# A planner that keeps GpSimd's time, and a multiply that moves to GpSimd, in a two-layer attention and MLP kernel

## The chip, the cores and the metric

The kernel runs on one core of one Trainium2 chip. A core has five engines that run side by side: TensorE (PE in the profile; its weight loads are PEld), VectorE (DVE), ScalarE (ACT), GpSimd (POOL) and SyncE (SP), which here only issues DMAs. Each engine takes its instructions in order. They share the on-chip memory SBUF; matmuls write to the banks of PSUM, which VectorE and ScalarE read. The metric is the device time of one execution in microseconds; the time given for a kernel is the median of several.

## The reference

Two layers, each with attention and an MLP with the same weights, on x of 2048 x 512. LN is a norm without scale or shift.

```python
for _ in range(2):
    qkv = LN(x) @ wqkv                       # 512 -> 3 x 32 heads x 16
    p = softmax(q @ k^T * 16 ** -0.5)        # per head, 2048 x 2048
    x = x + (p @ v, heads side by side) @ wo
    x = x + silu(LN(x) @ w1) @ w2            # 512 -> 1792 -> 512
```

There are 2 layers x 32 heads x 2048 x 2048 exponentials, and no mask.

## The kernel before

**Tiling.** Scores are made transposed: 128 keys (a key tile, 16 of them) by 512 queries (a chunk `qc`, 4 of them). A *step* is one key tile of one head group (`g`, `par`), which has four heads; their four score matmuls have a contraction of 16 and lie in four row strips of the array, so they run at once. A *run* is the steps of one head group over its key tiles: 16, or fewer where `RUNS` splits them (in the first chunk of layer 0 four runs of 4 steps, as keys become ready; steps 1 to 128). There are 1024 steps.

**Exponentials.** They are shared out. Of a step's four blocks, ScalarE takes three (one instruction for one block, one for two, L1140), in tiles `p_sb`. The fourth, the block `d`, goes another way and is scored four steps ahead (`D_LEAD`): VectorE turns the scores `d_ps` into 16-bit integers `d_y` (L1058) that, read as fp16, are a rough exponential, and GpSimd adds two constants to a pair of them (`d_z`, L1078, two instructions for two steps). The three terms are multiplied with weighted values (`VA`, and `VB`, which GpSimd makes in `scale_v`, L559) and their sum is a closer exponential. The first 12 steps differ: there four blocks go to ScalarE.

**PV.** Every second step, `emit_pv` (L933) multiplies the exponentials with the values into one PSUM bank `o_ps`, in which a run's sum is kept, with a row of ones for the softmax's denominator. It decides which of the waiting terms of `d` blocks it takes: term y from one step after it was issued, the z terms from three and four steps after, all that are left at a run's end or when buffers (five pairs) would run out.

**A run's end.** VectorE copies `o_ps` to `oT` (L1038). For 45 of the 64 head groups (`by_dma`) an SP transpose brings it to `ot`; then VectorE takes the reciprocal of the denominators (`rec`, L601) and multiplies (L603) into `attn`. For the other 19, TensorE transposes into PSUM (`att`) and the same two instructions read that. When a chunk's groups are done, `out_proj` issues four SP transposes out of `attn` and background work begins: output projection, norm, MLP, next layer's keys, values and queries.

**The planner.** All engines' instruction streams are written in one order by the Python code. Beside the fixed stream of steps stand generators of background work (`Background`: `queue`, `side`, `outs`, `urgent`). Each yields a `Part` with its cost on TensorE (`pe`) or VectorE (`dve`) and a label it needs. `Model` keeps a clock for TensorE (`pe`), ScalarE (`act`), VectorE (`dve`) and SP (`sp`), and after each step's exponentials the loop issues every part that `fits`: one whose work ends, by the model, before ScalarE would miss its next scores. `done[label]` is the modelled time at which a label is ready. GpSimd has no clock in it. Of the norms, `ln_stats` issues statistics on VectorE and two GpSimd instructions for `rstd` (L396, L397), and `ln_chunk` applies them on VectorE (`xn`, L402), in three buffers, and transposes them by SP.

**Zero multiplications.** In a step with no other TensorE work, `fill(FILL)` issues three groups of four matmuls of zeros into the open `o_ps`, if the model has room. It can't do this when the newest accumulation has not been started in all four column strips or is finished. `warm(n)` makes n matmuls into a bank of the background (`bank`, one bank after step 5).

**Tail.** After the last step come the last chunk's output projection, norm and MLP, by hand (`tail`).

Of the kernel before, what the change touches and what calls it, by code (L numbers as in the profile page):

```python
# [28 lines left out]
class Background:  # L29
# [44 lines left out]
    def advance(self, item):  # L74
        if self.model:
            self.model.charge(item[2])
        try:
# [4 lines left out]
            else:  # L82
                home = [q for q in (self.outs, self.side, self.queue) if item in q][0]
                home.remove(item)
                self.done[item[0]] = self.model.landed if self.model else 0.0

    def heads(self, now):
        return [
            self.outs[0] if self.outs else None,
            self.head(now),  # L90
            self.prime(self.side[0]) if self.side else None,
        ]
# [17 lines left out]
class Model:  # L110
# [12 lines left out]
    TRANSPOSED = 1.7  # L123
    DMA = 0.64

    def __init__(self, slack, margin):
        self.slack, self.margin = slack, margin
        self.pe = self.act = self.dve = self.ready = self.free = 0.0
        self.s1 = self.sd = self.copied = self.sp = self.landed = 0.0
        self.s2 = [0.0, 0.0]  # L130
        self.mode = None
        self.early = False
        self.evacuated = 0.0
# [37 lines left out]
    def pv(self, groups):  # L171
        self.pe = max(self.pe, self.copied)
        self.to("V")
        self.pe += self.GROUP * groups
        self.summed = self.pe + self.TO_DVE

    def transpose(self):
# [41 lines left out]
def kernel(  # L219
# [10 lines left out]
    nc = tc.nc  # L230
# [188 lines left out]
    def ln_pair(c, i):  # L419

        stats[c, i] = yield from ln_stats(c, (i, i + 1))

    def ln_transpose(i, xns, dst, copy=nc.vector.tensor_copy):
# [9 lines left out]
    def ln_chunk(c, dst):  # L433

        for i in (0, 2):
            mv, rstd = stats.pop((c, i))
            for u in range(2):
                yield part(0.45, need=("xn", xn_count[0] - XN_BUFS))
# [112 lines left out]
    def scale_v(L, c):  # L551

        n = len(d_blocks(c))
        VB[L, c] = vbpool.tile([P, n * 2 * VBW + 16], FP16, name="VB", tag="VB", bufs=7)
        nc.gpsimd.memset(VB[L, c][:, n * 2 * VBW :], 0.0)
# [17 lines left out]
    def group_out(L, qc, pi, g, par, oT):  # L573
# [10 lines left out]
        else:  # L584
# [16 lines left out]
        nc.vector.reciprocal(rec[:], att[:, :, :, 16:17])  # L601
        yield part(0.43, held=not by_dma(L, qc, pi, g, par))
        nc.vector.tensor_tensor(  # L603
            out=attn[L, qc][:, :, P * g : P * (g + 1)].rearrange(
# [29 lines left out]
    def out_proj(L, qc):  # L634
        if (L, qc) == (0, 0):
            load_wo()
        aT = wo[0][:, CT : 2 * CT, :].rearrange("p t (c q) -> p t c q", c=CT)
        for i in range(4):
            transpose(aT[:, i, :, :], attn[L, qc][:, i, :])
# [311 lines left out]
    def emit_pv(t, mms):  # L951
# [20 lines left out]
        for d in list(d_todo):  # L972
# [3 lines left out]
            must = ends or d["pair"] <= last  # L976
            while d["rhs"] and (must or d["rhs"][0][0] <= t):
                if must:
                    _, k, rhs = d["rhs"].pop(0)
                    lanes[j].append(pv_block(d["blk"], k, rhs))  # L980
                else:
                    more[j].append((d, d["rhs"].pop(0)))
# [67 lines left out]
    def emit_d(t, blk):  # L1050
# [14 lines left out]
        )  # L1065
        d = dict(blk=blk, pair=len(pairs), left=NT)
        d["rhs"] = [(t + 1, 0, pr["y"][:, len(pr["ds"]), :].bitcast(FP16))]
        pr["ds"].append(d)
# [4 lines left out]
    def other_terms(t, pr):  # L1073

        n = len(pr["ds"])
        for k, (off, _) in enumerate(TERMS):
# [7 lines left out]
                op1=ALU.mult,  # L1084
            )
            for i, d in enumerate(pr["ds"]):
                d["rhs"].append((t + 3 + k, k + 1, z[:, i, :].bitcast(FP16)))

    def end_group(L, qc, pi, g, par):
# [13 lines left out]
    with tc.manual_schedule(  # L1103
# [62 lines left out]
        for t in range(1, len(steps)):  # L1166
# [19 lines left out]
            for i in range(n1):  # L1186
                score(a_blks[i], s1[i])
            if n1 == 1:
                for blk in d_blks:
                    emit_d(t, blk)  # L1190
            m.scores(len(a_blks), len(d_blks))
            while after:
# [37 lines left out]
            if not busy and m.fill_fits(FILL):  # L1230
                n = fill(FILL)
                if n:
                    m.pv(n)
        t = len(steps) + 1
        emit_pv(t, pv_step(t))
# [37 lines left out]
```

## Time and profile before

| what | value |
|---|---|
| time, median of 4 executions | 1566.27 us (1563.36 to 1567.93) |
| the profiled execution's own time | 1563.36 us |
| its span, first to last instruction | 1561.6 us |
| ScalarE busy | 1513.9 us, 97% |
| TensorE busy (matmuls; zeros included) | 1458.2 us, 93% |
| GpSimd busy | 1113.8 us, 71% |
| VectorE busy | 1080.3 us, 69% |
| mean granted TensorE clock | 0.993 |
| first exponential of the stream; last step's first | 14.2 us; 1518.8 us |

The busy time of ScalarE counts overlapping instructions once. A row of the profile's groups gives line, engine, operation, output and inputs, shapes and count, then busy time and mean length of one, then the idle time of the engine just before them and what ended it. What ended a wait is inferred: it is the event that came last. In rows of stages the columns are the stretch, its length, each engine's busy time with the number of instructions, the granted clock, the DMA engines' share and GB/s.

### The profile page before, as it was taken

How to read it: one execution, taken by the hardware profiler on the slowest of the kernel's cores; microseconds unless marked ns; L12 is line 12 of the kernel's file. 1: busy time of each engine (PE TensorE's matmuls, PEld its weight loads, DVE VectorE, ACT ScalarE, POOL GpSimd, SP SyncE). 2: the span in 40 equal slices, each digit the busy share in tenths (PEclk: the TensorE clock that was granted, in tenths of full speed). 3: DMA queues.
4: the chain of work that ended last, by engine and by line, in shares of the span. 5: the costliest groups of instructions: out<-in, count | busy, mean ns of one | idle time of the engine just before them, and what ended most of it. 6: DMA issues, size and time to landing. Idle time of an engine off the chain costs nothing. (4 is left out here: it accounts for less than half of the span.)

```text
span 1561.6 us, 34164 instructions
## 1 busy us (share of the span) xinstructions
PE 1458.2 (93%) x13284; PEld 465.2 (30%) x13361; DVE 1080.3 (69%) x1733; ACT 1513.9 (97%) x2191; POOL 1113.8 (71%) x1172
## 2 busy tenths in 40 slices
PE   7999998899998999899998999988999899999998
PEld 3222332222322322222222323322332232222225
DVE  6877677667776777667776677676677666676645
ACT  6999999999999999999999999999999999999993
POOL 2888777677876778667876778776777677776760
PEclk9999999999999999999999999999999999999999
DMA  4110013101121112201021010121012101120110
GB/s 138 32 28 2 5 36 65 31 23 37 45 47 27 35 22 52 52 18 39 21 49 43 10 35 9 24 58 32 18 46 62 32 18 29 45 48 22 38 45 14
DMA packets 149442, 55.84 MB, mean 36 GB/s; under 512 B 127776, under 2 KB 148768, under 8 KB 149280
## 3 DMA queue, kind: packets, MB, share of 16 engines
q1 hardware_dynamic: 149280, 53.65, 14.1%
q8 instruction: 105, 1.72, 0.5%
q14 instruction: 57, 0.47, 0.1%
HBM read 28.57 MB, written 4.19 MB: 21 GB/s over the span
## 5 line engine op out<-in xcount | busy, mean ns | idle before, releaser
L1140 ACT ACTIVATE p_sb<-s_ps 128x512 bf16<-128x512 f32 x2026 | 1467.0, 1104 | 7.3 <-PE d_ps L909 6.2
L1078 POOL TENSOR_SCALAR d_z<-d_y 128x1024 uint16<-128x1024 uint16 x1012 | 1058.0, 1045 | 366.6 <-DVE d_y L1058 179.2
L1058 DVE TENSOR_SCALAR d_y<-d_ps 128x512 uint16<-128x512 f32 x1012 | 696.9, 689 | 404.0 <-PE d_ps L909 360.4
L909 PE MATMUL s_ps<-QT,KT 32*128 32x512 bf16 x3084 | 631.1, 382 | 61.4 <-ACT p_sb L1140 45.1
L909 PE MATMUL d_ps<-QT,KT 32*128 32x512 bf16 x1012 | 389.8, 385 | 8.4 <-DVE d_y L1058 5.2
L909 PEld LDWEIGHTS <-KT 32*128 32x128 bf16 x4096 | 187.4, 91 | 647.8 <-issue 595.2
L933 PE MATMUL o_ps<-p_sb,VA 128*32 128x512 bf16 x3039 | 311.9, 388 | 8.0 <-DVE oB L1038 1.1
L933 PE MATMUL o_ps<-d_z,VB 128*32 128x512 f16 x2024 | 249.4, 381 | 0.0
L933 PE MATMUL o_ps<-d_y,VA 128*32 128x512 f16 x1012 | 153.4, 380 | 0.0
L933 PEld LDWEIGHTS <-VA 128*32 128x32 bf16 x4096 | 86.6, 95 | 159.6 <-issue 121.9
L466 PE MATMUL h_ps<-fT,w 128*128 128x512 bf16 x392 | 102.6, 382 | 8.4 <-DVE hT L652 6.6
L711 PE MATMUL f_ps<-w_sb,hT 128*128 128x512 bf16 x350 | 97.0, 382 | 4.1 <-issue 3.3
L933 PEld LDWEIGHTS <-VB 128*32 128x32 f16 x2024 | 78.5, 98 | 55.4 <-issue 0.5
L933 PE MATMUL o_ps<-w_qkv,zero 128*32 128x512 bf16 x1344 | 93.1, 383 | 0.0
L649 ACT ACTIVATE t_sb<-h_ps 128x512 f32<-128x512 f32 x98 | 86.7, 884 | 0.0
L652 DVE SCALAR_TENSOR_TENSOR hT<-t_sb,h_ps 128x512 bf16<-128x512 f32 x98 | 67.2, 686 | 22.8 <-ACT t_sb L649 22.6
L603 DVE TENSOR_TENSOR attn<-ot,rec 128x256 bf16<-128x256 bf16 x45 | 49.5, 1099 | 1.5
L1038 DVE CAST oT<-o_ps 128x512 bf16<-128x512 f32 x64 | 43.5, 680 | 7.7 <-PE o_ps L933 7.7
L466 PEld LDWEIGHTS <-w 128*128 128x128 bf16 x392 | 30.0, 97 | 55.1 <-issue 30.3
L402 DVE TENSOR_SCALAR xn<-x,mv,rstd 128x512 bf16<-128x512 bf16 x64 | 42.5, 677 | 3.5 <-POOL rstd L397 1.9
L392 DVE BATCH_NORM_STATS2 st<-x 128x6 f32<-128x512 bf16 x64 | 43.5, 680 | 2.0 <-DMA x<-in_A_x_dram 2.0
L711 PEld LDWEIGHTS <-hT 128*128 128x128 bf16 x392 | 29.2, 97 | 46.4 <-issue 25.0
(77 smaller groups left out, 613.8 us busy)
## 6 DMA issues: line engine op xcount, KB each, us to landing
w<-in_B_w_dram SPq DMA_DIRECT2D x100, 128.0 KB, 2.4
wo<-in_A_wo_dram SPq DMA_DIRECT2D x8, 512.0 KB, 3.7
QT<-q SPq DMA_DIRECT2D x240, 16.0 KB, 1.8
x<-in_A_x_dram SPq DMA_DIRECT2D x7, 512.0 KB, 4.2
x<-x SPq DMA_DIRECT2D x16, 128.0 KB, 1.8
x<-x SPq DMA_DIRECT2D x4, 512.0 KB, 3.7
out_dram<-x SPq DMA_DIRECT2D x16, 128.0 KB, 1.7
w_sb<-in_B_w_dram SPq DMA_DIRECT2D x1, 1792.0 KB, 13.5
```

The costliest lines, as they stand in the source:

```text
L392: nc.vector.bn_stats(st[:], x_sb[c][:, i, :])
L466: nc.tensor.matmul(ps.rearrange("p (t q) -> p t q", q=P) if len(r.shape) == 3 else ps, lhsT=lhs(ct), rhs=r, start=(ct == 0), stop=(ct == C ...
L603: nc.vector.tensor_tensor(out=attn[L, qc][:, :, P * g : P * (g + 1)].rearrange("p t (j s) -> p t j s", s=32)[:, :, :, 16 * par : 16 * par ...
L649: nc.scalar.activation(t_sb, h_ps, ACT.Tanh, scale=0.5)
L652: nc.vector.scalar_tensor_tensor(out=hT[:, ft, :], in0=t_sb, scalar=1.0, in1=h_ps, op0=ALU.add, op1=ALU.mult)
L711: nc.tensor.matmul(y_ps, lhsT=hT[:, ft, tq * P : (tq + 1) * P], rhs=w2_sb[:, ft, :], start=(ft == 0), stop=(ft == FT - 1),)
L909: nc.tensor.matmul(out, lhsT=KT[L, kt // 4][r, g, (kt % 4) * P : (kt % 4 + 1) * P], rhs=QT[g][r, par, :], start=True, stop=True,)
L933: nc.tensor.matmul(o_tiles[key][32 * j : 32 * j + 32, :], lhsT=lhsT, rhs=rhs, start=(o_count[key][j] == 0), stop=stop,)
L1038: nc.vector.tensor_copy(out=o, in_=o_tiles[key][:])
L1058: nc.vector.tensor_scalar(out=pr["y"][:, len(pr["ds"]), :], in0=s_ps[:], scalar1=float(1024 * SCALE * math.log2(math.e)), scalar2=float(10 ...
L1078: nc.gpsimd.tensor_scalar(out=z[:, 0:n, :].rearrange("p a b -> p (a b)"), in0=pr["y"][:, 0:n, :].rearrange("p a b -> p (a b)"), scalar1=fl ...
L1140: nc.scalar.activation(p_sb, s_ps, ACT.Exp, bias=-SHIFT * math.log(2.0) + math.log(EXP_SUM), scale=float(SCALE),)
```

## The change

`Model` gets a clock for GpSimd, `pool`. `pool_busy(us)` starts at the later of GpSimd's clock and VectorE's plus 0.1, adds the cost and returns when the result may be used. It is charged for `rstd` (1.0), the scaled values (2.6), each `d_z` instruction (0.65 or 1.1) and the new multiply (0.62).

It is used in three places. `ln_chunk` waits for the modelled `rstd` before `xn` is issued. From step 128 on, `emit_pv` takes a waiting term ahead of its deadline only if the model has it ready (`d["ready"]`); so that the model's VectorE clock is right, `m.scores` now comes before `emit_d`. And SP's modelled clock waits for the last `scaled` multiply before the transposes out of `attn`.

The multiply at L603 moves from VectorE to GpSimd where the data comes by DMA (45 of 64); there its part of 0.43 on VectorE is dropped. The reciprocal stays on VectorE.

Last, where `fill` returns nothing after step 5, the background bank is free by the model and no background part is half done, `warm(FILL)` issues three matmuls.

```diff
+    def idle(self):
+        return self.active is None and not any(i[2] is not None and i[2].held for i in self.queue)
 ...
+    ADD = {1: 0.65, 2: 1.1}
 ...
+    def pool_busy(self, us):
+        self.pool = max(self.pool, self.dve + 0.1) + us
+        return self.pool + 0.1
 ...
         stats[c, i] = yield from ln_stats(c, (i, i + 1))
+        bg.done["rstd", c, i] = bg.model.pool_busy(1.0) if bg.model else 0.0
 ...
             mv, rstd = stats.pop((c, i))
+            yield part(need=("rstd", c, i))
 ...
         n = len(d_blocks(c))
+        if bg.model:
+            bg.model.pool_busy(2.6)
 ...
-        yield part(0.43, held=not by_dma(L, qc, pi, g, par))
-        nc.vector.tensor_tensor(
+        if by_dma(L, qc, pi, g, par):
+            scale = nc.gpsimd.tensor_tensor
+            bg.model.scaled = bg.model.pool_busy(0.62)
+        else:
+            yield part(0.43, held=True)
+            scale = nc.vector.tensor_tensor
+        scale(
 ...
+        bg.model.sp = max(bg.model.sp, bg.model.scaled)
         for i in range(4):
             transpose(aT[:, i, :, :], attn[L, qc][:, i, :])
 ...
-            while d["rhs"] and (must or d["rhs"][0][0] <= t):
+            while d["rhs"] and (
+                must or d["rhs"][0][0] <= t and (t < 8 * NKT or d["ready"][d["rhs"][0][1]] <= m.pe)
+            ):
 ...
+        d["ready"] = [m.dve + 0.1]
 ...
+            ready = bg.model.pool_busy(bg.model.ADD[n])
             for i, d in enumerate(pr["ds"]):
                 d["rhs"].append((t + 3 + k, k + 1, z[:, i, :].bitcast(FP16)))
+                d["ready"].append(ready)
 ...
+            m.scores(len(a_blks), len(d_blks))
             if n1 == 1:
                 for blk in d_blks:
                     emit_d(t, blk)
-            m.scores(len(a_blks), len(d_blks))
 ...
             if not busy and m.fill_fits(FILL):
                 n = fill(FILL)
                 if n:
                     m.pv(n)
+                elif t > 5 and m.free <= m.pe and bg.idle():
+                    warm(FILL)
+                    m.to("B")
+                    m.pe += m.GROUP * FILL
```

More of the change, by code (lines that the diff above doesn't have):

```diff
@@ L128, in __init__ @@
         self.pe = self.act = self.dve = self.ready = self.free = 0.0
-        self.s1 = self.sd = self.copied = self.sp = self.landed = 0.0
+        self.s1 = self.sd = self.copied = self.sp = self.landed = self.pool = 0.0
         self.s2 = [0.0, 0.0]
         self.mode = None
+        self.scaled = 0.0
         self.early = False
```

## The prediction

> **What bounds the kernel now.** I read the profiled execution in this order: the page's busy times, stage windows, who ScalarE waited for, the timeline of the worst places, and then the rows of the operation that moves.
>
> The page's first part (busy us, share of the span, instructions):
> ```profile
> PE 1458.2 (93%) x13284; PEld 465.2 (30%) x13361; DVE 1080.3 (69%) x1733; ACT 1513.9 (97%) x2191; POOL 1113.8 (71%) x1172
> ```
> ScalarE is the bound. GpSimd has 1561.6 - 1113.8 = 447.8 us idle. The table of stages (length, busy time of each engine with instructions, granted TensorE clock, DMA):
> ```profile
> core 0: us, PE busy (x) PEld busy (x) DVE busy (x) ACT busy (x) POOL busy (x), PEclk, DMA share, GB/s
> ...
> 32.00:48.00 16.00, 13.05 (x76) 2.20 (x75) 10.27 (x21) 12.54 (x19) 9.77 (x12) 0.57 0.29 68
> ...
> 84.00:92.00 8.00, 6.61 (x48) 1.37 (x45) 5.71 (x10) 6.53 (x10) 7.04 (x7) 0.79 0.37 98
> ...
> 248.00:254.00 6.00, 4.47 (x55) 1.17 (x44) 3.44 (x6) 4.74 (x7) 3.38 (x4) 1.00 0.87 107
> ...
> 1047.00:1052.00 5.00, 3.23 (x41) 0.96 (x42) 3.97 (x6) 4.08 (x7) 2.14 (x2) 1.00 0.28 63
> ...
> 1203.00:1208.00 5.00, 4.24 (x27) 0.90 (x28) 2.49 (x5) 3.78 (x7) 2.57 (x3) 0.66 0.01 3
> 1208.00:1520.80 312.80, 294.72 (x2816) 90.08 (x2831) 197.55 (x301) 312.69 (x452) 221.93 (x215) 1.00 0.14 35
> 1520.80:1562.00 41.20, 34.48 (x238) 21.07 (x242) 22.94 (x52) 13.68 (x31) 1.85 (x4) 1.00 0.04 14
> ```
> Read the ACT column against the length. From 1208 to 1520.8 us ScalarE idles 0.11 us. Its idle time inside the stream (16 to 1520 us) sits in a few places: 3.46 us in 32 to 48, 1.47 in 84 to 92, 1.22 at 253, and 0.44, 0.25, 0.17, 0.88 and 1.22 at 267.7, 455.1, 642.4, 1051.3 and 1205.4 to 1207.3. With crumbs that is 9.3 us. The head (16 us) and the tail (41 us) are written out by hand and untouched. So nothing in the change can win more than 9.3 us, 0.6%. Who ScalarE waited for (us, times, longest):
> ```profile
> ACT p_sb L1140 <- PE d_ps L909: 6.2, 10, 1.2
> ...
> ACT p_z L1140 <- PE s_ps L909: 1.9, 5, 0.9
> ```
> Scores came late. The timeline shows why (start, us, engine, line, op):
> ```profile
> 1047.43 0.69 DVE L1058 TENSOR_SCALAR d_y<-d_ps 128x512 uint16<-128x512 f32 x1 [1.51 <-PE d_ps L909]
> ...
> 1048.04 0.24 DVE L601 RECIPROCAL rec<-ot 128x16 f32<-128x16 bf16 x1
> ...
> 1048.28 2.22 POOL L1078 TENSOR_SCALAR d_z<-d_y 128x1024 uint16<-128x1024 uint16 x2 [2.00 <-DVE rec L601]
> 1048.32 1.28 DVE L603 TENSOR_TENSOR attn<-ot,rec 128x256 bf16<-128x256 bf16 x1
> 1049.52 0.67 DVE L652 SCALAR_TENSOR_TENSOR hT<-t_sb,h_ps 128x512 bf16<-128x512 f32 x1
> ...
> 1050.34 0.59 PE L466 MATMUL h_ps<-fT,w 128*128 128x512 bf16 x2 [1.77 <-DVE hT L652]
> ...
> 1051.32 0.60 ACT L1140 ACTIVATE p_sb<-s_ps 128x512 bf16<-128x512 f32 x1 [0.88 <-PE d_ps L909]
> ```
> The multiply at L603 starts beside a GpSimd `d_z` and takes 1.28 us where the planner charged 0.43. `hT`, which frees the only background PSUM bank, stands behind it on VectorE; the next `h_ps` matmul stands 1.77 us at the head of TensorE's queue; the scores behind it are late; ScalarE idles 0.88 us. The same sequence (rec, multiply of 1.28, hT, h_ps, scores) stands at 267.7, 455.1 and 642.4. At 1201.7 it cost a clock window too: 1203.7 to 1207.1 ran at half clock. The moved operation's rows (min/median/max ns):
> ```profile
> L603 DVE TENSOR_TENSOR attn<-ot,rec x45: 426/1275/1278, 236.7 to 1505.7; 128x256 bf16<-128x256 bf16 x45
> ...
> L603 DVE TENSOR_TENSOR attn<-att,rec x19: 411/424/425, 173.7 to 1523.1; 128x256 bf16<-128x256 f32 x19
> ```
> 35 of the 45 take over 1.2 us; the 19 that read PSUM never do. Last, two GpSimd groups (busy us, mean ns):
> ```profile
> L1078 POOL TENSOR_SCALAR d_z<-d_y 128x1024 uint16<-128x1024 uint16 x1012 | 1058.0, 1045 | 366.6 <-DVE d_y L1058 179.2 <-PE o_ps L933 109.4 <-DVE rec L601 21.9
> ...
> L559 POOL TENSOR_SCALAR VB<-VA 128x136 f16<-128x136 bf16 x64 | 19.5, 304 | 15.1 <-DVE VA L540 11.7
> ```
>
> **The change, part by part.**
>
> *The multiply moves to GpSimd.* Removed from VectorE: 45 instructions, 49.5 us. In 40 places other work covers that; in five it did not, and these return 0.44 + 0.25 + 0.17 + 0.88 + 1.22 = 2.96 us. The reciprocal (0.24) stays, so `hT` at 1049.52 could start about 1.2 us earlier, more than the 0.88 that ScalarE lost; what is next late there is the scores' own banks, which ScalarE frees. Added on GpSimd: no row shows this operation there. The two rows above give (1045 - 304) / (1024 - 136) = 0.83 ns per element and 190 ns fixed. Lower end: 256 elements as one input, 0.40 us. Upper end: the short-run rate of the VB row, 304/136 = 2.24 ns, for each of two inputs: 2 x 256 x 2.24 = 1.15 us. I take two inputs at 0.83, 0.62 us, because runs and sizes lie between the rows. 45 x 0.62 = 28 us (18 to 52) out of 448 idle. On the path: a `d_z` pair (2.17 us) comes every 2.77 us, so GpSimd falls behind by up to 1.15 us and has it back in two pairs. Readers of `d_z`: matching the matmuls that read z with the instructions that wrote it, in order, the smallest distance from z's end to its matmul is 3.0 us anywhere, the median 7. So 0 at either end; without that cover, each of 45 would cost at most 1.15, 52 us. The multiply waits for the reciprocal in GpSimd's queue, with the next `d_z` behind it; the reciprocal follows a `d_y` on VectorE at once, and GpSimd is then in a pair, so 0. The four transposes out of `attn` (28 on SP before the tail) wait for GpSimd instead of VectorE, seven times, at most a pair and the multiply, 2.8 us, with weight and q loads behind them; the model now charges it, the output projection comes later in background time, and each such stretch has zero fills left (24 to 96 of their matmuls per 25 us). I take 0; bounds 0 and 7 x 0.5 (ScalarE would see the part of 2.8 that a step of 1.4 and its buffers do not hide), 3.5 us.
>
> The Trainium skill (GPSIMD Engine Reference, Engine selection) speaks against this move: elementwise work with two inputs belongs on VectorE, GpSimd being about twice as slow. By it the multiply would take 2 x 0.424 = 0.85 us here, but the trace's VectorE row is 1.275, not 0.424, so by the row the move is a gain even on the operation alone; the sum by either is the same, since GpSimd is not on the path.
>
> *Norms.* `ln_chunk` now holds `xn` until the modelled `rstd` (0.24 + 0.71 us on GpSimd, charged 1.0). VectorE stood for `rstd` four times, 1.9 us in all. One place reached ScalarE: at 33.88 `xn` waited 0.61 us, the `d_y` behind it came at 34.21, and ScalarE idled 0.94 before 35.56. I take 0.6 back (bounds 0 and 0.94). Cost: `xn` slips up to one step (1.4 us) in 30 norm pairs; between the last norm of layer 0 (912.6) and the use of its keys (step 633 at 945.7) lie 33 us, of which the chain takes 13 to its first keys and 28 to its last values. Cost 0 while that holds; if it were gone, 1.4 us once.
>
> *PV terms.* A z term is taken only if the model has it ready, from step 128 on. With 3.0 us the smallest distance in the trace, the gate rarely closes; it changes which step a term is in, not how many matmuls there are (3036 read d_y or d_z before and after). 0; bounds: no gain, since no z was ever late; if 8 value scalings (2.4 us each on GpSimd) each push one group (0.217) into a full step, 1.7 us. Reordering `emit_d` and `m.scores` issues the same instructions.
>
> *Warm matmuls.* In a step without other TensorE work, where zeros have no open accumulation, three matmuls now run on the background bank. The trace has 15 such steps: two in 32 to 40, where the model has no room (a `d` score waits for ScalarE's third bank), and 13 at 152 to 169, 914 to 987, 1141, 1313 to 1335 and 1477 to 1500. All 13 ran at clock 1.00 without an idle ScalarE, so the gain is 0; the 8.5 us of TensorE (13 x 3 x 0.217) lie in its idle time, as the 1344 zero matmuls do. Bounds: 0 and, if VectorE is late in freeing the bank each time, 13 x 0.69 = 9.0 us.
>
> On the clock the page TensorE: Matmul & The Clock Gate (HAM oscillation) says that idle gaps over about 3.4 us let it fall. This trace differs: it fell after 1200.2 to 1203.7, where TensorE was 61% busy and no gap passed 1.06 us. By the page, warm matmuls would gain nothing; by the trace they could where busy shares are 0.6, but none of those places is among the 13.
>
> **Sum.** 2.96 + 0.6 = 3.6 us off the profiled execution: 1563.36 (span 1561.6 and 1.8 around it) to 1559.8. That execution was the fastest of four; the median is 2.9 above it. The windows of the clock lie differently in each run, and half of the ten low stretches of TensorE (under 0.68 busy in 3.4 us) are the five multiplies. An estimate: half of 2.9, 1.45, would go with them; I take half of that, 0.7. So 1566.27 - 3.6 - 0.7 = 1562.0.
>
> **Rivals.**
>
> *New collisions in `xn` (slower).* `xn`, 42.5 us in all, still costs 0.45 in the planner and took 0.94 to 1.24 us in 22 of 64. At 82.8 two in a row (2.36 us) cost 1.47; at 249.8 one late for its buffer cost 1.22. Every placement shifts now, so new ones may arise. At 1.35 each, three cancel the gain; six put it at 1562.0 + 8.1 = 1570.1, slower by over 0.2%. For: `xn` already made the two largest late stalls. Against: only two of 64 did, and a VectorE with 49.5 us less has room.
>
> *No change.* The five stalls return in other places or GpSimd's multiply makes `xn` wait in their stead: two or three collisions, 1566. For: the shortened queue pulls `hT` and `xn` earlier, beside other `d_z`. Against: `hT` takes 0.67 to 0.69 beside `d_z` as well as without.
>
> *More.* The half-clock stretch of 32 to 48 goes too, since `xn` no longer delays the `d_y` there: another 2.9, and 84 to 92 with it, 1.5: 1557.6. For: the clock fell after a stretch 0.63 busy. Against: at steps 9 to 12 TensorE has little work in either version.
>
> **How the numbers follow.** Forecast 0.50, no change 0.27, collisions 0.15, more 0.08. About 0.2%, 3.1 us, is what a measurement of this kernel tells from none. Faster means below 1563.1: nearly all of "more" and four fifths of the forecast's 1559.5 to 1564.5, 0.48; slower the 0.15 and little else, 0.16; same the rest, 0.36. The likeliest range is 1559.5 to 1564.5; 8 in 10 reach from 1557 (more) to 1569.5 (just over the slower bound).
>
> **What would show it.** Right: 45 multiplies on GpSimd at 0.4 to 1.15 us; no ScalarE idle with rec and hT before it; VectorE busy near 1031; no xn standing for rstd; `z` matmuls never waiting; 39 or so warm matmuls. Wrong: ScalarE idle over 10 us in the stream, with `xn`, SP's transposes or a warm matmul ahead of it; or `d_z` under its readers by less than 0.5 us.

## The result and the profile after

The changed kernel takes 1568.87 us (median; 1564.58 to 1576.05), the kernel before beside it 1565.37 (1561.94 to 1568.68). The ratio is 1.0021, interval 1.0015 to 1.0027: slower by 0.21%, 3.3 us. The time lies inside the wide predicted range (1557 to 1569.5) and above the likeliest one (1559.5 to 1564.5); the forecast was 4.3 us faster, so the sign was wrong. The profiled execution took 1566.94 us with a span of 1565.2, 3.6 more than before in both.

The profile page of the changed kernel, first part (busy us, share of the span, instructions):

```profile
PE 1470.9 (94%) x13310; PEld 472.5 (30%) x13406; DVE 1033.8 (66%) x1688; ACT 1513.9 (97%) x2191; POOL 1139.1 (73%) x1217
```

VectorE lost 46.5 us of work, GpSimd gained 25.3, and ScalarE, the bound, works exactly as long as before. All of the 3.6 us are therefore idle time of ScalarE. The row of the moved operation (min/median/max ns):

```profile
L621 POOL TENSOR_TENSOR attn<-ot,rec x45: 617/620/624, 238.6 to 1511.3; 128x256 bf16<-128x256 bf16 x45
```

The estimate was 0.62 us. Where did the time go? The windows of the changed kernel (stretch, its length, then each engine's busy time):

```profile
32.00:48.00 16.00, 13.89 (x84) 2.35 (x87) 11.30 (x22) 13.12 (x20) 10.27 (x13) 0.57 0.27 68
...
250.00:258.00 8.00, 6.64 (x42) 1.44 (x42) 3.70 (x6) 4.00 (x6) 2.96 (x3) 0.57 0.18 35
...
1047.00:1052.00 5.00, 4.28 (x38) 1.31 (x31) 3.33 (x7) 5.00 (x10) 3.85 (x5) 1.00 0.35 79
1203.00:1208.00 5.00, 4.15 (x40) 1.25 (x40) 3.45 (x5) 5.00 (x9) 3.23 (x4) 1.00 0.23 53
...
200.00:750.00 550.00, 515.38 (x4662) 160.55 (x4696) 364.95 (x590) 541.42 (x782) 417.14 (x440) 0.99 0.18 38
750.00:1522.00 772.00, 736.69 (x6844) 231.23 (x6878) 499.90 (x792) 772.00 (x1116) 579.73 (x591) 1.00 0.14 34
```

The same two long windows of the kernel before:

```profile
200.00:750.00 550.00, 517.86 (x4752) 160.71 (x4780) 393.02 (x618) 547.84 (x792) 409.66 (x423) 1.00 0.16 38
750.00:1520.00 770.00, 725.24 (x6748) 225.02 (x6783) 518.95 (x809) 767.82 (x1109) 562.59 (x564) 1.00 0.14 34
```

Read the fourth busy column, ScalarE. At 1047 and 1203, where the multiply had stalled it, it is now busy without a gap (5.00 of 5.00), and from 750 us to the end of the stream it idles 0.00 us instead of 2.18. But from 200 to 750 us, the background work of layer 0, it idles 550 - 541.42 = 8.58 us instead of 2.16. Who waited for a DMA, in the changed kernel (us, times, longest us):

```profile
PEld L477 <- DMA w<-in_B_w_dram: 3.8, 3, 2.1
DVE rec L614 <- DMA ot<-oT: 3.6, 3, 2.0
DVE xn L411 <- DMA fT<-xn: 3.3, 1, 3.3
PE h_ps L477 <- DMA w<-in_B_w_dram: 3.0, 2, 1.8
PE k_ps L477 <- DMA xnT<-xn: 2.4, 3, 1.1
```

And in the kernel before:

```profile
PEld L466 <- DMA w<-in_B_w_dram: 2.5, 5, 1.1
...
DVE xn L402 <- DMA fT<-xn: 1.4, 1, 1.4
DVE rec L601 <- DMA ot<-oT: 0.7, 2, 0.4
```

Of the new places where ScalarE is late (253.9 to 258.0, 444.0, 454.6, 528.4, 560.0, 633 to 644, 747 to 750) all but two have one of these waits ahead of them. At 444.0 and at 633.4 no DMA is waited for: two `xn` in a row run beside `d_z` on GpSimd and hold back the next `d_y`. The row ahead of 444.0:

```profile
439.68 1.98 DVE L411 TENSOR_SCALAR xn<-x,mv,rstd 128x512 bf16<-128x512 bf16 x2
```

The largest place in the timeline of the changed kernel (start, us, engine, line, operation, in brackets the idle time before and what ended it), SP's own queue first:

```profile
237.88 5.25 SPq L528 DMA_DIRECT2D QT<-q  x8
243.18 0.57 SPq L327 DMA_DIRECT2D x<-in_A_x_dram  x1
243.80 1.04 SPq L698 DMA_DIRECT2D w<-in_B_w_dram  x2
244.96 6.96 SPq L317 DMA_TRANSPOSE fT<-xn  x4
```

```profile
250.29 0.41 DVE L411 TENSOR_SCALAR xn<-x,mv,rstd 128x512 bf16<-128x512 bf16 x1 [3.26 <-DMA fT<-xn]
250.62 0.68 DVE L1079 TENSOR_SCALAR d_y<-d_ps 128x512 uint16<-128x512 f32 x1
251.35 0.58 PE L928 MATMUL d_ps<-QT,KT 32*128 32x512 bf16 x1 [2.28 <-DVE d_y L1079]
...
253.95 1.51 ACT L1164 ACTIVATE p_sb<-s_ps 128x512 bf16<-128x512 f32 x2 [2.97 <-PE d_ps L928]
```

`xn` has three buffers, and the fourth `xn` of a chunk needs the first one's transpose to have left its buffer. The transposes stand on SP behind eight q loads, a load of `x` of 512 KB and two of `w`. The row of 6.96 us holds all four and, before the fourth, SP's own wait for the fourth `xn`. The first starts at 244.96 and lands at 250.19, 5.2 us later, the longest of the 28 into `fT` (in the kernel before it took 3.9):

```profile
DMA to landing us min/median/max: 2.4/2.4/5.2
```

The planner charges 1.27 for one and takes it to land 1.7 us later, 2.97 after its start, which is late for the median and early for this one; it charges nothing for the load of `x` and for the first loads of `w`. So it issues `xn` where it thinks the buffer is free; `xn` stands 3.26 us in VectorE's queue, `d_y` behind it, the next `d` scores behind that, and ScalarE idles 2.97 us. The granted clock is 0.57 in this window.

Over the whole stream the two traces can be set against each other instruction by instruction. ScalarE's instructions overlap: the following rows (kernel before, ScalarE's timeline) show one of 1.37 us, then one 0.90 us after its start, and one 0.48 us after that.

```profile
450.12 1.37 ACT L1140 ACTIVATE p_sb<-s_ps 128x1024 bf16<-128x1024 f32 x1
451.02 0.96 ACT L649 ACTIVATE t_sb<-h_ps 128x512 f32<-128x512 f32 x1
451.50 2.38 ACT L1140 ACTIVATE p_sb<-s_ps 128x512 bf16<-128x512 f32 x3
```

So I count a *late start*: how much later than 0.903 us (after a 1024-wide row) or 0.476 us (after a 512-wide one) the next row starts. Summed over the stream that is 41.67 us before and 45.25 after, a difference of 3.58, the whole of the loss. After 200 us, single late starts of 0.25 us or more sum to 9.31 before and 13.16 after; 11.4 of the 13.16 have a wait for a DMA ahead of them.

### The profile page after: what moved, and what is told of

Read it like the earlier page. It is cut to its first block, busy times and chain, and to the rows that moved or that the text cites. A ratio compares the mean times of both kernels' runs of the same rounds, so it can differ in the third digit from the quotient of the medians.

```text
span 1565.2 us, 34295 instructions
## 1 busy us (share of the span) xinstructions
PE 1470.9 (94%) x13310; PEld 472.5 (30%) x13406; DVE 1033.8 (66%) x1688; ACT 1513.9 (97%) x2191; POOL 1139.1 (73%) x1217
## 3 DMA queue, kind: packets, MB, share of 16 engines
q8 instruction: 105, 1.72, 0.4%
## 5 line engine op out<-in xcount | busy, mean ns | idle before, releaser
L928 PE MATMUL s_ps<-QT,KT 32*128 32x512 bf16 x3084 | 644.0, 382 | 51.0 <-ACT p_sb L1164 37.1
L928 PEld LDWEIGHTS <-KT 32*128 32x128 bf16 x4096 | 190.7, 91 | 649.3 <-issue 601.3
L952 PE MATMUL o_ps<-d_z,VB 128*32 128x512 f16 x2024 | 249.5, 381 | 0.0
L477 PE MATMUL k_ps<-xnT,w_qkv 128*128 128x512 bf16 x128 | 35.4, 389 | 3.4 <-DMA xnT<-xn 2.4
```

The lines of the kernel that those rows point to most:

```text
L477: nc.tensor.matmul(ps.rearrange("p (t q) -> p t q", q=P) if len(r.shape) == 3 else ps, lhsT=lhs(ct), rhs=r, start=(ct == 0), stop=(ct == C ...
L928: nc.tensor.matmul(out, lhsT=KT[L, kt // 4][r, g, (kt % 4) * P : (kt % 4 + 1) * P], rhs=QT[g][r, par, :], start=True, stop=True,)
L952: nc.tensor.matmul(o_tiles[key][32 * j : 32 * j + 32, :], lhsT=lhsT, rhs=rhs, start=(o_count[key][j] == 0), stop=stop,)
```

## The experiments

Two theories stand against each other. *Landings*: the new placement puts background work ahead of DMA landings that the planner believes done, because its clock of SP runs ahead of the real queue; the multiply's move itself pays as predicted. *Luck*: any re-placement makes some forced or unlucky places, and this one drew more of them. Some expectations state further theories of their own. Times in them are differences of medians; below I compare ratios to the kernel before (run beside each), and 0.001 is 1.57 us. Two kernels are surely apart only where their intervals do not overlap.

| run | kernel | median us | ratio | interval |
|---|---|---|---|---|
| | changed kernel | 1568.87 | 1.0021 | 1.0015 to 1.0027 |
| 1 | before + GpSimd multiply | 1559.76 | 0.9961 | 0.9949 to 0.9974 |
| 2 | before, multiply not charged | 1564.98 | 0.9995 | 0.9983 to 1.0006 |
| 3 | changed, multiply on VectorE | 1565.99 | 1.0004 | 0.9993 to 1.0016 |
| 4 | multiply and its charges alone | 1563.41 | 0.9989 | 0.9977 to 1.0001 |
| 5 | changed, no wait for rstd | 1566.48 | 1.0009 | 1.0001 to 1.0018 |
| 6 | changed, no SP charge | 1562.40 | 0.9978 | 0.9969 to 0.9988 |
| 7 | changed, no warm matmuls | 1573.25 | 1.0056 | 1.0044 to 1.0069 |
| 8 | changed, four `xn` buffers | 1565.72 | 1.0006 | 0.9996 to 1.0015 |
| 9 | changed, landings charged | 1564.40 | 1.0000 | 0.9990 to 1.0010 |
| 10 | run 1 + warm | 1561.36 | 0.9974 | 0.9963 to 0.9985 |
| 11 | run 10, landings charged | 1575.85 | 1.0069 | 1.0053 to 1.0085 |
| 12 | run 4 + warm | 1562.77 | 0.9987 | 0.9978 to 0.9996 |
| 13 | changed, landings charged from step 128 | 1557.87 | 0.9947 | 0.9929 to 0.9965 |
| 14 | run 13 without warm | 1559.68 | 0.9954 | 0.9938 to 0.9970 |
| 15 | run 1, landings charged from step 128 | 1577.30 | 1.0066 | 1.0050 to 1.0082 |
| 16 | run 13 without the SP charge | 1557.83 | 0.9959 | 0.9945 to 0.9972 |
| 17 | run 13, multiply on VectorE | 1585.59 | 1.0138 | 1.0120 to 1.0157 |

### The move alone, and the charge alone

Run 1 keeps the order of the kernel before on every engine and changes the multiply's engine only:

```diff
-        nc.vector.tensor_tensor(
+        (nc.gpsimd if by_dma(L, qc, pi, g, par) else nc.vector).tensor_tensor(
```

> The kernel before with one edit: the 45 multiplies run on GpSimd, and the planner still charges VectorE 0.43 us for each, so that every instruction of TensorE, ScalarE and SP stays in its place. Theory P (the move itself returns what the prediction said, and the loss comes from the new placement that the dropped 0.43 and the new labels lead to): the five stalls behind the multiply (0.44, 0.25, 0.17, 0.88, 1.22) vanish and nothing comes instead: about 3 us under before, ratio 0.998. Rival G (the multiply on GpSimd itself costs: z terms late, VectorE held off): same as or slower than before, ratio 1.000 to 1.002.

Measured: 0.9961, 6.1 us faster (5.3 by medians). The five stalls behind the multiply are gone; ScalarE's idle time from 200 to 750 us is 550 - 548.67 = 1.33 us. Who waited for a DMA there is close to the kernel before:

```profile
DVE rec L601 <- DMA ot<-oT: 1.5, 3, 0.7
DVE xn L402 <- DMA fT<-xn: 1.2, 1, 1.2
```

So the move is worth more than forecast, and the rest of the change takes back some 9 us (1.0021 - 0.9961). Run 2 leaves the multiply on VectorE and drops its charge:

```diff
-        yield part(0.43, held=not by_dma(L, qc, pi, g, par))
+        yield part(0.0 if by_dma(L, qc, pi, g, par) else 0.43, held=not by_dma(L, qc, pi, g, par))
```

> The kernel before with one edit: the multiplies stay on VectorE, but the planner charges nothing for them instead of 0.43 us. Theory P: waits for DMA landings appear in layer 0 (xn, rec, k_ps, h_ps), as in the changed kernel, and the multiply's own stalls stay or grow: 4 to 8 us over before, ratio 1.0025 to 1.005. Rival G: 45 times 0.43 us too little charged shows only as more stalls behind the multiply, no DMA waits; ratio about 1.001.

0.9995: a new placement with the stalls in other places, and no difference that can be told. Both theories had it slower, and the waits for landings that theory P expected did not come (`xn` waits 1.1 us for `fT`, 1.4 in the kernel before).

### Parts taken out of the change

Run 3 puts the multiply back on VectorE with its charge of 0.43. The wait for `rstd`, the gate of PV terms and the warm matmuls stay; the line on SP's clock stays too but does nothing, since `scaled` is set only where the multiply runs on GpSimd:

```diff
-        if by_dma(L, qc, pi, g, par):
-            scale = nc.gpsimd.tensor_tensor
-            bg.model.scaled = bg.model.pool_busy(0.62)
-        else:
-            yield part(0.43, held=True)
-            scale = nc.vector.tensor_tensor
+        yield part(0.43, held=not by_dma(L, qc, pi, g, par))
+        scale = nc.vector.tensor_tensor
```

> The changed kernel with the multiply back on VectorE and charged 0.43 us: norms, PV terms and warm matmuls stay. Theory P: within 1.5 us of before (the 0.6 us of the norms may show). Rival W (warm matmuls or the wait for rstd cost the time): about 3 us over before, ratio 1.002.

1.0004. The stall at 253 us is here too (late starts 2.86 and 1.03) with the multiply's five in their old places. The parts that act here cost nothing that can be told beside the kernel before; they are not the whole rest of the change, as SP's line is without effect.

Run 4 is the multiply on GpSimd with its charges, without the wait for `rstd`, the line on `bg.model.sp`, the gate of PV terms and the warm matmuls:

```diff
-            yield part(need=("rstd", c, i))
 ...
-        bg.model.sp = max(bg.model.sp, bg.model.scaled)
 ...
-                must or d["rhs"][0][0] <= t and (t < 8 * NKT or d["ready"][d["rhs"][0][1]] <= m.pe)
+                must or d["rhs"][0][0] <= t
 ...
-                elif t > 5 and m.free <= m.pe and bg.idle():
-                    warm(FILL)
-                    m.to("B")
-                    m.pe += m.GROUP * FILL
```

> The changed kernel without the wait for rstd, without warm matmuls and without SP's charge for the multiply: the multiply moves and its 0.43 us is dropped, nothing else. Theory P: slower than before by 2 to 5 us with waits for DMA landings in layer 0, as the changed kernel. Rival W: about 3 us faster than before.

0.9989, 5.0 us below the changed kernel and 4.4 above run 1, which differs from it in the placement alone: there the multiply kept 0.43 us of the planner's VectorE time. Their intervals do not overlap, so the dropped charge takes back most of the 6.1 us that the move wins. Theory P had run 4 slower than the kernel before, the rival some 3 us faster; it is 1.7 us faster, with an interval that just holds 1. Run 5 takes out only the first of these lines, run 6 only the second, run 7 only the last four.

> The changed kernel without the wait of xn for the modelled rstd. Its TensorE, ScalarE and SP orders stay but for a few rows; VectorE's differs in the first chunk and around four later norms, one of them at 250 us. Theory N (the wait places the fourth xn of the first MLP norm one step earlier, ahead of a d_y, where it stands for a transpose's landing): the 4.0 us of ScalarE's idle time at 254 to 258 shrink to under 1.5, the 0.5 at 34 us comes back: 2 to 3 us under the changed kernel, ratio to before about 1.0003. Rival S (SP's charge is the cause): no change, ratio 1.002.

> The changed kernel without the line by which SP's modelled clock waits for the last multiply. Theory S (this charge moves output projection, MLP, q copies and transposes against each other from 250 us on, so that the waits for landings at 444, 455, 528, 560, 636, 644, 747 and 750 arise, 4.5 us in all): 3 to 5 us under the changed kernel, ratio to before 0.9990 to 1.0003. Rival N: the stall at 254 stays and with it most of the loss, ratio 1.001 to 1.002.

> The changed kernel without the 38 warm matmuls in the stream; VectorE's and ScalarE's orders are the same to the row. Theories N and S: same as the changed kernel within 0.7 us, ratio to before 1.002. Rival W (warm matmuls hold TensorE or the clock): 3 us under it, ratio 1.000.

Run 5: 1.9 us below the changed kernel, with intervals that just overlap; the late start at 253.5 us falls from 3.44 + 0.97 to 1.73, and the waits in the other chunks stay. The fourth `xn` still waits 2.3 us for `fT` here, and 2.7 and 2.4 in runs 10 and 12, which have no wait for `rstd` either (3.3 in the changed kernel, 1.4 in the kernel before). So the norms' wait lengthens this stall and is not its only source.

Run 6: 6.7 us below, the largest single part. The waits for `w` at 454 and 642 us and for `ot` at 528 are gone; the stall at 253 stays (idle 2.9), as it must: VectorE's instructions stand in the changed kernel's order up to 418 us. Who waited for a DMA in run 6, to be set against the five rows of the changed kernel:

```profile
DVE xn L411 <- DMA fT<-xn: 3.2, 1, 3.2
...
DVE rec L614 <- DMA ot<-oT: 1.8, 3, 1.0
PE k_ps L477 <- DMA xnT<-xn: 1.7, 3, 0.7
...
PEld L477 <- DMA w<-in_B_w_dram: 0.2, 1, 0.2
```

Run 7: 5.5 us *above*. The instruction orders of VectorE and ScalarE are those of the changed kernel; only the warm matmuls are missing. (The expectations speak of 13 places, as the prediction did. The changed kernel has 19, 57 matmuls of which 38 are in the trace: the 13 forecast, and six more in layer 0, at 354.5, 399.6, 543.4, 589.1, 732.1 and 778.9 us.) The same waits are longer (`h_ps` for `w` 5.1 us instead of 3.0, `k_ps` for `xnT` 3.9 instead of 2.4), and instead of one half-clock stretch after 200 us there are eight, at 249.5, 369.0, 454.3, 645.5, 754.7, 928.8, 980.0 and 1003.9 us. So the warm matmuls are worth something in this placement. Why the waits at landings are longer without them is not shown; for three of the stretches the runs below show more.

Run 10 adds the warm matmuls to run 1, where they come in the 13 places of the prediction, and run 12 adds them, and the gate, to run 4:

```diff
+                elif t > 5 and m.free <= m.pe and bg.idle():
+                    warm(FILL)
+                    m.to("B")
+                    m.pe += m.GROUP * FILL
```

> The kernel of e1 (before, multiply on GpSimd, placement kept) with the warm matmuls of the change added. It tells what the warm matmuls are worth by themselves. Prediction's step (0): same as e1 within 0.7 us, 1559.8 us. Theory H (they hold the clock over the whole kernel, as taking them from the changed kernel cost 4 us): 2 to 4 us under e1, 1556 to 1558 us.

> The changed kernel without the wait for rstd and without SP's charge: multiply, gate on PV terms and warm matmuls. Theories N and S together: the stall at 254 (4 us) and the waits that SP's charge leads to (5 us) are both gone, 1560 to 1562 us. If the two parts' costs do not add: 1562 to 1566 us.

In run 10 they cost 2.0 us, with intervals that overlap, and a late start of 3.13 us at 255.1 where run 1 has 1.37 at 252.8; in run 12 they change 0.3 us. In runs 7 and 10 ScalarE, VectorE and GpSimd have the same instructions in the same order as in the kernel beside them, so the warm matmuls change times and the clock there, not the placement.

What they do to the clock can be read from four pairs of kernels that differ in them: run 7 and the changed kernel, runs 1 and 10, 4 and 12, and 14 and 13 (below). With warm matmuls no half-clock stretch begins within 6 us of any of their 73 places. Without them one begins 1.3 to 2.9 us after 7 of the 73: at 928.8, 980.0 and 1003.9 in run 7, 1312.3 in run 1, 587.7 and 775.4 in run 4, and 441.6 in run 14. No DMA is waited for ahead of those of runs 1 and 7. The windows of 3.4 us before two of them (run 1, then run 7), in which TensorE was busy for 80 and 75%:

```profile
1308.90:1312.30 3.40, 2.71 (x28) 0.79 (x29) 1.98 (x3) 3.40 (x7) 2.62 (x3) 1.00 0.04 10
```

```profile
1000.50:1003.90 3.40, 2.55 (x32) 0.60 (x20) 2.26 (x4) 3.40 (x7) 2.09 (x2) 1.00 0.13 33
```

The late starts behind run 7's three sum to 2.5 us. These are counts from one trace of each kernel.

### The landings themselves

Run 8 gives `xn` a fourth buffer (`bufs=4`, `XN_BUFS = 4`) in the changed kernel, so that the fourth `xn` no longer waits for a transpose.

> The changed kernel with four xn buffers in place of three, in the pool and in the planner, so that the fourth xn never waits for the first transpose. Theory D (waits for DMA landings that the planner places too early are what costs; the largest is xn's at 250 us): the 4.0 us at 254 to 258 go, the other waits stay: 3 to 4 us under the changed kernel, ratio to before 0.9995 to 1.0003. Rival (the stall at 254 has another cause, such as TensorE's clock): no change.

2.3 us below the changed kernel, the intervals just touching. The stall at 254 is gone, as the cause named above says it must be, and others are larger: `PEld` for `w` 5.3 us instead of 3.8, an idle of 1.51 us at 451.5, and late starts of 1.60 and 1.72 us at 38.4 and 41.5. Curing one wait leaves the planner's clock wrong for the next.

Run 9 makes the clock more cautious, by charging the uncharged loads and by a margin: with 2.7 a transpose is taken to land 3.97 us after its start, where the measured median is 2.4 and the longest 5.2. I call this the corrected clock.

```diff
-    TRANSPOSED = 1.7
+    TRANSPOSED = 2.7
 ...
             nc.sync.dma_start(x_sb[c][:, i : i + n, :], src[:, i : i + n, :])
+            if bg.model:
+                bg.model.dma(1)
 ...
+                bg.model.dma(1)
+                bg.done["w", self.key, ft] = bg.model.sp + 2.3
 ...
         for ft in range(FT):
+            yield part(need=("w", (L, c), ft))
             w = w1.get(ft)
```

> The changed kernel, all parts kept, with SP's modelled clock made truer: x loads and every w load charged 0.64 us when they are issued, each w given a label (SP's clock + 2.3 us) that its matmuls wait for, and a transpose's landing put 1.0 us later (2.7 in place of 1.7). Theory D (the loss is work issued ahead of DMA landings that the planner puts too early): the waits for w, xnT, fT and ot shrink from 13 us to under 5 in all, 5 to 9 us under the changed kernel, ratio to before 0.996 to 0.999. Rival L (any new placement loses by chance as much as it gains): the waits come back in other places, 1564 to 1569 us.

1.0000, 3.3 us below the changed kernel, less than hoped. After 200 us the late starts of 0.25 us or more fall from 13.16 to 1.60 us. But one new stall stands in the first chunk, where the later landings hold back the keys until a step needs them (timeline of run 9):

```profile
80.67 0.69 DVE L500 CAST KT<-k_ps 128x512 bf16<-128x512 f32 x1 [5.25 <-PE k_ps L479]
81.08 1.51 ACT L1168 ACTIVATE p_sb<-s_ps 128x512 bf16<-128x512 f32 x2 [5.12 <-PE s_ps L932]
```

Both theories can claim this: the waits at landings went, and a forced place came. Run 11, the same clock on run 10, speaks for luck: 1.0069 with 14.8 us of late starts from 956 to 991 us, where the landings theory had the fastest kernel of all.

> The kernel of e10 with the truer clock of SP of e9. Theory D: fewer waits than e10, 1555 to 1559 us, the fastest of all. Rival L: the new placement loses what it gains, 1559 to 1564 us.

Run 13 tests the two theories on the changed kernel without that forced place: the corrected clock from step 128 on only, so that the first 200 us keep their order.

```diff
+            if t == 128:
+                m.TRANSPOSED = 2.7
```

(with `TRANSPOSED` 1.7 until then and the loads of `x` uncharged until then, the rest as in run 9).

> The changed kernel with the planner's clock of SP corrected as in the ninth run (x and w1 loads charged, w1 waited for, a transpose taken to land 2.7 us after SP instead of 1.7), but only from step 128 on, the end of the first chunk, so that the first 200 us keep the changed kernel's order. Landings theory (the changed kernel is slow because its planner puts work ahead of DMA landings in layer 0): the stall of 5.3 us at 81.1 us and the 1.5 us behind it, which the ninth run's new clock made in the first chunk, do not come, and ScalarE still starts late by under 3 us in all after 200 us; 1564.4 less 6.8 gives 1557 to 1560, below the engine's move alone (1559.8) or level with it. Rival (every new placement makes a forced place somewhere, and the changed kernel merely drew a bad one): another single stall of several us turns up elsewhere, and the time is 1562 to 1569.

0.9947, the lowest ratio of this study: 11.6 us below the changed kernel and 8.3 below the kernel before, as the landings theory had it. It beats both kernels; from run 1, which does too, its interval does not part it. Its windows:

```profile
200.00:750.00 550.00, 523.68 (x4740) 165.18 (x4773) 371.63 (x601) 549.86 (x796) 424.27 (x447) 1.00 0.18 38
750.00:1514.00 764.00, 729.38 (x6758) 229.47 (x6804) 493.41 (x781) 764.00 (x1105) 572.69 (x585) 1.00 0.15 34
```

ScalarE idles 0.14 us from 200 us to the end of the stream (8.58 in the changed kernel), and late starts of 0.25 us or more after 200 us sum to 1.66. The larger ones that are left lie before 100 us. So the changed kernel's loss sat at its landings, and a placement that avoids them gives it back.

Runs 14 and 16 take the warm matmuls and the SP charge out of run 13.

> The run before without the 13 early zero multiplications. If they help only by keeping TensorE's clock full through the stalls at the DMA landings, there is nothing left for them to do once those stalls are gone: within 1.5 us of the run before, and no more half-clock stretches than it has. If the clock drops wherever a piece is without background work, stall or none: 3 to 5 us slower than the run before, as it was without them in the changed kernel (4.4), with about ten half-clock stretches.

> The thirteenth run without the line that makes the planner's clock of SP wait for GpSimd's multiply. Landings theory: that line cost 6.5 us in the changed kernel only because it moved work ahead of landings; with the landings charged it may stay or go: within 1.5 us of the thirteenth run (0.9947 of the kernel before), late starts of ScalarE after 200 us under 4 us. Rival (the line itself, as a truer clock or a worse one, decides): 3 to 7 us away from it, on either side.

0.9954 and 0.9959, 1.1 and 1.9 us above run 13 with intervals that overlap. The SP charge, 6.7 us in the changed kernel, and the warm matmuls, 5.5 there, are worth nothing that can be told once the planner is cautious about landings. The line also moves little then: ScalarE's order is the same in runs 9, 13, 14 and 16, and VectorE's in run 16 leaves run 13's only at 789 us. These four are thus one placement and not four draws. Run 14 has a half-clock stretch that run 13 lacks (441.6 us, with a late start of 1.47 us at 444.4 instead of 0.60), which its expectation had ruled out.

Runs 15 and 17 show what the corrected clock needs. Run 15 is run 1 with it; run 17 is run 13 with the multiply back on VectorE and its charge of 0.43 (and so, as in run 3, with SP's line without effect).

> The kernel before with the multiply on GpSimd alone (1559.8), and the corrected clock of SP from step 128 on. Landings theory: its remaining waits for transposes and w1 in layer 0 (some 3 us of late starts after 200 us) go, 1557 to 1559.5. Rival: a re-placement is as likely to make a new forced place, as the eleventh run did at 957 to 989 us: 1561 to 1575.

> The thirteenth run with the multiply of the head outputs back on VectorE (charged 0.43 us there). If the move itself is what pays once no work is put ahead of a landing: slower than the thirteenth run by 4 to 6 us, as before against the engine alone (5.3), with the stalls behind the multiply back in layer 1 (about 1050 and 1205 us). If the better clock of SP is what pays: within 2 us of it.

1.0066 and 1.0138: slower than the kernel before by 10.3 and 21.6 us. Both are misses: the landings theory had run 15 at 1557 to 1559.5 us, and run 17 was put 4 to 6 us above run 13. In run 17 the sequence of the prediction is back with full price at 289.4, 1092.2 and 1437.0 us (timeline of run 17 at one of them):

```profile
1088.55 2.22 POOL L1104 TENSOR_SCALAR d_z<-d_y 128x1024 uint16<-128x1024 uint16 x2 [1.14 <-DVE rec L616]
1088.59 1.28 DVE L623 TENSOR_TENSOR attn<-ot,rec 128x256 bf16<-128x256 bf16 x1
...
1090.61 1.01 PE L479 MATMUL h_ps<-fT,w 128*128 128x512 bf16 x2 [1.06 <-DVE hT L673]
...
1092.23 1.51 ACT L1168 ACTIVATE p_sb<-s_ps 128x512 bf16<-128x512 f32 x2 [0.80 <-PE d_ps L932]
```

And all three kernels that have the corrected clock together with the charge of 0.43 (runs 11, 15 and 17) stall where layer 1 begins: 14.8, 16.3 and 15.5 us of late starts between 956 and 996 us. Who waited there, in run 17 (950 to 1000 us):

```profile
ACT p_sb L1168 <- PE s_ps L932: 7.7, 2, 5.3
ACT p_sb L1168 <- PE d_ps L932: 6.5, 3, 5.1
DVE KT L500 <- PE k_ps L479: 5.3, 1, 5.3
PE d_ps L932 <- DMA QT<-q: 4.1, 1, 4.1
```

The keys and queries of layer 1 come late, and a step that needs them waits for the whole chain. The four kernels with the clock and without the charge (9, 13, 14, 16) show no late start of 0.25 us there. My reading is that 45 parts of 0.43 us and later landings together make the background fall behind its due times; that chain of reasons was not tested further. So the corrected clock is no gain by itself: it led to two orders of ScalarE's work (one in runs 9, 13, 14 and 16, the other in 11, 15 and 17), and only the first is fast. That this one came by luck is not ruled out.

## Why the prediction failed, point by point

**The multiply: right in mechanism, mis-sized.** 45 instructions at 0.62 us, z never late (smallest distance 2.85 us, forecast bound 3.0), VectorE at 1033.8 (forecast near 1031), the five stalls gone. The term "return 0.44 + 0.25 + 0.17 + 0.88 + 1.22 = 2.96 us" measured 6.1 us in run 1 by ratio and 5.3 by medians; the two profiled executions differ by 3.6. It summed ScalarE's idle time. The row of a 1024-wide exponential lasts 1.371 us, but the next can start after 0.903, so 0.47 us of every stall lie under the row of the instruction before and are not idle. By late starts the five places cost 0.81 + 0.72 + 0.64 + 1.04 + 1.27 + 0.53 = 5.01 us, and three more at 364.6, 552.0 and 739.3 us, where the multiply stood in the way too, cost 0.38 each with next to no idle time (0.02 or less): 6.15 in all, and none of these is left in run 1. But a half-clock stretch at 1312.3 us (late starts of 0.97) and smaller late starts come in their stead, and over the stream the sum falls by 3.65 us only; that 6.15 meets the 6.1 of the ratio is in part luck. For the same reason "nothing in the change can win more" does not follow from 9.3 us of idle time: after 200 us the kernel before idles 4.34 us (2.16 + 2.18), and run 13's late starts there, all sizes together, are 5.4 us fewer.

**The dropped charge: no term at all.** The prediction gives the 0.43 us that the planner no longer charges no price. Run 4 against run 1 puts the placement that follows from it at 4.4 us; with the multiply on VectorE (run 2) it costs nothing that can be told.

**SP's clock: the step that failed.** "The four transposes out of `attn` ... wait for GpSimd instead of VectorE ... I take 0; bounds 0 and 3.5 us." I priced the real wait of SP's queue. The edit's effect was another: it moves the planner's clock, and with it where background parts are issued (from 418 us on in VectorE's order). Run 6 puts this line at 6.7 us, outside the bounds. The transposes wait for GpSimd's multiply with the line and without it, so it is not this wait that run 6 takes away but the placement ahead of landings: its waits for `w` at 454 and 642 us go. Run 16 agrees: with the corrected clock the line moves little and costs nothing that can be told.

**Norms: gain right, cost wrong.** At 34 to 36 us late starts fell from 1.46 to 0.96, near the 0.6 taken. "Cost 0 while that holds" looked at the distance between the last norm and the use of its keys. The price lay elsewhere: `xn` stood longer for its buffer behind SP's queue at 250 us, 1.9 us by run 5, with intervals that overlap. The rival "New collisions in `xn`" named this place and its wait (one late for its buffer at 249.8) and the sign; it did not say that the change itself would lengthen it. Its other cause, `xn` made longer beside GpSimd, came true at 444.0 and 633.4, with late starts of 0.80 and 0.58 us.

**PV terms: right.** The gate never closes; with and without it the instruction streams are the same.

**Warm: price wrong, and six places missed.** The 13 forecast places are there, and six in layer 0 that the new placement left without TensorE work. "All 13 ran at clock 1.00 without an idle ScalarE, so the gain is 0" took one trace for all: without warm matmuls the clock fell behind such places in runs 1, 4, 7 and 14. Run 7 puts them at 5.5 us, of which 2.5 stand behind three of the 13 places; the rest lies mostly at waits for landings. Run 10 (2.0 us the other way, with intervals that overlap) and run 14 (nothing that can be told) give them no fixed price.

**Clock, -0.7 estimated.** The half-clock stretch at 1203.7 us went with its stall, as assumed, but a longer one (6.8 us from 250.7) came with the new stall. I had counted only what the old stalls would take away with them.

**What would show it wrong** was stated rightly: "ScalarE idle over 10 us in the stream, with `xn`, SP's transposes ... ahead of it". It idles 13.1 us, 8.6 of them after 200 us and mostly with these ahead. I gave that case 0.15, priced its collisions at 1.35 us each and had no term for the planner's landings, though the trace before shows the row `xn` for the DMA of `fT` with 1.4 us and the DMA share of 0.87 at 248 to 254.

## What to carry to other kernels

Where a planner places work, an edit of its clock moves everything behind it: price such an edit not by the wait it describes but by asking which of the planner's clocks is already ahead of its queue, and what would then be issued too early. Before making a planner stricter on one resource, compare its modelled landings with the traced ones; here a more cautious clock turned a change of +0.21% into one of -0.53%. It is no recipe: the same clock made run 1 slower (0.9961 to 1.0066), so each placement has to be measured. Size a stall of a pipelined engine by the start-to-start time of its instructions, not by its idle time.

## What the runs showed of the hardware

- ScalarE overlaps its instructions by nearly half a microsecond: a 128x1024 exponential lasts 1.371 us in the trace and the next starts as early as 0.903 us after its start, 0.468 of overlap; after a 128x512 one, 0.476 us. The Trainium skill (ScalarE: Activation LUTs, What ACT_TABLE_LOAD costs) says back-to-back activations overlap by about 93 ns; here the measured 468 decides. A stall of up to 0.47 us is therefore invisible as idle time.
- A two-input bf16 multiply of 128x256 takes 0.620 us on GpSimd in every one of 45 places (617 to 624 ns), while on VectorE it took 1.275 where it started beside a `d_z` of GpSimd (the median), 0.426 at least, and from PSUM 0.424. The Trainium skill (GPSIMD Engine Reference, Engine selection) has GpSimd at about half of VectorE's speed for two inputs; against the 0.424 the ratio here is 1.5, and against the row that the kernel really had the move gained.
- A DMA transpose into `fT` landed 5.2 us after its start behind eight q loads, a load of 512 KB and two of 128 KB, where the median of the 28 in the changed kernel is 2.4.
- Between 200 us and the end of the stream, half-clock stretches came where work stood for DMAs (250.7 us in the changed kernel, beside a matmul's wait of 2.28 us; five of the eight in run 7), and also with no DMA waited for and TensorE busy for 75 to 80% of the 3.4 us before, where a step was left without zero or warm matmuls (three in run 7, one in run 1). Run 13, which has neither, shows none. At the stalls, which causes which was not separated.
